# Rows of tiles 4 and 5 through HBM, own PSUM banks for the halves of the first scores and transposes, one buffer for the last output, and a list drawn up anew

## The chip, the cores and the metric

The kernel runs on one core of a Trainium2 chip. The metric is the device time of one execution in microseconds (us), lower is better; it is the median of several executions. TensorE (PE) does the matrix products and the transposes, VectorE (DVE), ScalarE (ACT) and GpSimd (POOL) do the element-wise work, SyncE (SP) issues most of the DMAs, and ACT issues the others. Each engine runs its own instructions in the order of the program.

## The reference

The first part is an attention with a window: for each of 4 batches, 8 heads, 768 positions and 64 columns per head, a query sees the keys nearer than 16 positions and, besides, one summary of each block of 32 positions (the maximum of the keys, the mean of the values). The second part is a two-layer network on the 3072 rows that come out. Cut to what matters:

```python
k_sum = k.reshape(B, H, nb, 32, D).max(axis=3)
v_sum = v.reshape(B, H, nb, 32, D).mean(axis=3)
scores_l = where(|i - j| < 16, scale * q @ k.T, -1e9)
scores_s = scale * q @ k_sum.T + log(32)
a = softmax(concat([scores_l, scores_s]))
x = a @ concat([v, v_sum])            # 3072 rows of 512
h = x @ w_in                          # 512 -> 1024
solu = h * softmax(h)
ln = (solu - mean(solu)) / sqrt(var(solu) + 1e-6) * g_ln
out = ln @ w_out                      # 1024 -> 512
```

All of it is float32. A product of the network is made as three products of rounded parts (high times low, low times high, high times high), so one 128x512 piece is a group of three matmuls.

## The kernel before, in words

The rows are worked on in 24 tiles of 128 rows. One step of the attention, named by batch, part and pair as in `s0_1_0`, makes the rows of half the heads of two tiles: scores `s` (PE), masked and reduced by DVE to `e` and its maximum `nm`, `exp` on ACT with the sums `z`, a division (DVE or POOL), transposes `t` (PE), copies `at` (ACT or DVE), and products with the values `vt` and the block means `vsum` to `x`. The rows are split into a high and a low part, `xh` and `xl`. A tile's first layer is `h` (8 groups of three matmuls; from tile 8 on two tiles are combined into `hu`, `hl` and `hf`), then softmax and normalisation give `he`, and the second layer `o` (8 groups) needs `he` transposed, in the parts `lh` and `ll`. Its result is scaled to `os` by ACT or DVE, and ACT issues the store.

The transposition of `he` has two forms. Tiles 0 to 5 are turned by PE into PSUM (`lt`, line 1130), and ACT and DVE split them from there. Tiles from `FAR_FROM` on are turned in 32x32 blocks by DVE (`tbl`, line 1086), sent to HBM (`farl`, line 1090), fetched back by four DMAs that put the blocks in place (line 1096), and split out of SBUF.

At the start the weights have to be rounded as well: each of 8 pieces of `w_in` (`raw`, `cv`, `w`) takes some seven operations on ACT, DVE and POOL before PE can use it, and the 8 pieces of `w_out` the same.

Nothing of the order is decided on the chip. A planner records each operation with its engine and what it depends on; the table `ORDER` lists all 1890 operations in the order in which the engines get them, `OTHERS` says which run on another engine than the first choice. The planner's own costs serve for one thing only: where they leave PE without work before 80 us, it puts in products of zeros (line 1353, called fillers here), so that PE does not idle. Buffers are rings: a new `s` or `t` takes one of two slots of two PSUM banks each, and must wait until the last tile of that slot is done with.

Of the kernel before, what the change touches and what calls it, by code (L numbers as in the profile page):

```python
# [1397 lines left out]
```

## Time and profile before

| | us |
|---|---|
| median of 3 executions (lowest, highest) | 358.99 (358.83, 360.65) |
| profiled execution | 358.75 |
| span of the profiled execution | 357.0 |
| PE busy in the span | 348.5 |
| DVE busy | 293.2 |
| ACT busy | 264.3 |
| POOL busy | 189.5 |
| DMA moved | 67.80 MB |

The profiled execution's own time is 1.75 us over its span; that part lies outside the rows of the trace. Busy time is a sum over stages with different limits, so it is read stage by stage below.

### The profile page before, as it was taken

What the parts mean: (1) busy time and instruction counts of PE and PEld (TensorE: products, weight loads), DVE (VectorE), ACT (ScalarE), POOL (GpSimd) and SP (SyncE); (2) the same over time, 40 slices, a digit from 0 to 9 for tenths busy, and PEclk for the clock granted to TensorE, in tenths of its full rate; (3) what the DMA queues carried; (4) which work ended last, traced back from release to release, by engine and by line L of the source; (5) the groups of instructions that cost most, each with busy time, mean ns of one, the idle gap of its engine ahead of it and who ended that gap; (6) DMA issues with size and microseconds to landing.
All of it is one profiled execution on the core that took longest, in us unless ns stands there. A gap on an engine that the chain in (4) does not pass through costs nothing.

```text
span 357.0 us, 9393 instructions
## 1 busy us (share of the span) xinstructions
PE 348.5 (98%) x3305; PEld 274.9 (77%) x3311; DVE 293.2 (82%) x969; ACT 264.3 (74%) x780; POOL 189.5 (53%) x330
## 2 busy tenths in 40 slices
PE   8699999999999999999999999999999999999995
PEld 3446667878878888788888888888888888888885
DVE  3889999989899999896878797987988888848421
ACT  4879999978879887889888497797786866654210
POOL 5723446594869859467786345265233353511430
PEclk9999999999999999999999999999999999999999
DMA  7999933745214456286494565683474352354611
GB/s 263 414 413 408 409 142 109 270 119 172 106 46 130 153 206 194 86 287 198 159 311 135 169 211 173 202 251 114 135 228 180 119 170 103 137 176 159 213 70 59
DMA packets 28314, 67.80 MB, mean 190 GB/s; under 512 B 3828, under 2 KB 13300, under 8 KB 26732
## 3 DMA queue, kind: packets, MB, share of 16 engines
q1 hardware_dynamic: 24668, 60.92, 50.2%
q10 hardware_dynamic: 3600, 6.29, 5.0%
q8 instruction: 26, 0.43, 0.5%
q14 instruction: 20, 0.16, 0.2%
HBM read 49.55 MB, written 15.73 MB: 183 GB/s over the span
## 4 chain that ended last, share of the span: by engine, by line
PE 90%; DVE 5%; DMA 2%; issue 1%; ACT 1%; SPq 0%; POOL 0%; DVEq 0%
PE o L1156 37%; PE hu L980 12%; PE h L960 12%; PE x L800 6%; PE hl L980 6%; PE s L676 6%; PE t L741 3%; PE hf L980 3%; DMA kraw<-in_k 2%; DVE e L697 1%; PE vs_ps L557 1%; PE lt L741 1%; DVE ksum L537 1%; DMA out<-os 1%; PE vs_ps L570 1%
## 5 line engine op out<-in xcount | busy, mean ns | idle before, releaser
L1156 PE MATMUL o<-w,lh 128*128 128x512 f32 (+1 forms) x400 | 132.0, 386 | 0.0
L1156 PEld LDWEIGHTS o<-w,lh 128*128 128x128 f32 x400 | 74.1, 188 | 15.6 <-issue 0.5
L1156 PE MATMUL o<-w,ll 128*128 128x512 f32 (+1 forms) x200 | 76.2, 381 | 0.0
L709 ACT ACTIVATE e<-e,nm 128x120 f32<-128x120 f32 x192 | 73.2, 387 | 0.9 <-DVE nm L697 0.8
L960 PE MATMUL h<-w,xh 128*128 128x512 f32 x128 | 44.1, 399 | 0.0
L697 DVE CUSTOM_DVE_ANT_0 e<-s,mask 128x120 f32<-128x120 f32 x192 | 40.7, 276 | 3.4 <-PE s L676 3.4
L1156 PEld LDWEIGHTS o<-w,ll 128*128 128x128 f32 x200 | 37.6, 188 | 6.7
L376 POOL TENSOR_TENSOR ll<-lt,lh 128x512 fp32r<-128x512 f32 x17 | 22.6, 1329 | 37.6 <-ACT lh L368 21.7
L709 ACT ACTIVATION_READ_ACCUMULATOR e<-e,nm 128x1 f32 x192 | 36.9, 192 | 0.0
L960 PEld LDWEIGHTS h<-w,xh 128*128 128x128 f32 x128 | 24.0, 188 | 6.8 <-ACT at L368 0.8
L368 ACT COPY at<-t 120x512 f32<-120x512 f32 x37 | 20.2, 586 | 9.5 <-PE t L741 9.0
L800 PEld LDWEIGHTS x<-at,vt 120*64 120x64 f32 (+1 forms) x768 | 23.9, 138 | 3.8 <-issue 2.9
L1066 ACT ACTIVATE sq<-he 128x1024 bf16<-128x1024 f32 x24 | 25.3, 1055 | 1.8 <-DVE he L1061 0.8
L800 PE MATMUL x<-at,vt 120*64 120x64 f32 (+1 forms) x768 | 26.1, 224 | 0.2 <-POOL cv L476 0.2
L1043 ACT ACTIVATE he<-hs,hm 128x512 f32<-128x512 f32 x24 | 17.2, 718 | 11.8 <-DVE hm L1033 11.8
L1059 POOL TENSOR_SCALAR he<-he,nmu 128x512 f32<-128x512 f32 x19 | 13.5, 714 | 22.4 <-DVE nmu L1054 22.1
L960 PE MATMUL h<-w,xl 128*128 128x512 f32 x64 | 25.0, 391 | 0.0
L368 ACT CAST lh<-lt 128x512 fp32r<-128x512 f32 x35 | 20.5, 610 | 5.9 <-PE o L1156 4.7
L1162 ACT ACTIVATE os<-o,y 128x512 f32<-128x512 f32 x17 | 11.5, 685 | 14.8 <-issue 8.0
L1086 DVE STREAM_TRANSPOSE tbl<-he 128x1024 f32<-128x1024 f32 x18 | 22.3, 1237 | 0.1
L599 POOL TENSOR_TENSOR st_v<-st_v 96x512 f32<-96x512 f32 (+3 forms) x28 | 22.0, 789 | 0.4
L676 PE MATMUL s<-kw,qt 64*64 64x120 f32 x704 | 21.7, 267 | 0.1
(180 smaller groups left out, 842.7 us busy)
## 6 DMA issues: line engine op xcount, KB each, us to landing
vt<-in_v SPq DMA_DIRECT2D x12, 1024.0 KB
farl<-tbl SPq DMA_DIRECT2D x18, 512.0 KB
lt<-farl SPq DMA_DIRECT2D x72, 128.0 KB
kraw<-in_k SPq DMA_DIRECT2D x16, 400.0 KB
out<-os ACTq DMA_DIRECT2D x23, 256.0 KB
qt<-in_q SPq DMA_DIRECT2D x11, 512.0 KB
raw<-in_w_in SPq DMA_DIRECT2D x8, 512.0 KB
raw<-in_w_out SPq DMA_DIRECT2D x8, 512.0 KB
```

The lines of the kernel that those rows point to most:

```text
L368: by = {act: lambda: nc.scalar.copy(out=to(), in_=of()), dve: lambda: nc.vector.tensor_copy(out=to(), in_=of()), pool: lambda: nc.gpsimd.t ...
L376: pool: lambda: nc.gpsimd.tensor_tensor(out=to(), in0=a(), in1=b(), op=kind)}
L599: op(pool, 0.15 + w * 0.0021, lambda w=w, o=o: nc.gpsimd.tensor_tensor(out=o.ap[:n, :w], in0=x.ap[:n, :w], in1=x.ap[:n, w:2 * w], op=ALU.add),
L676: nc.tensor.matmul(sc.ap[cu * QT:(cu + 1) * QT, j, c:c + ks.shape[-1]], qs.ap[ds, 2 * pp + i, u * QT:(u + 1) * QT], ks, start=True, stop=True)
L697: nc.vector.tensor_tensor_reduce(out=e.ap[:, n, :], in0=sc.ap[:, j, (2 * i + up) * KC:(2 * i + up + 1) * KC], in1=mask[:, mi, :], scale=-S ...
L709: nc.scalar.activation(out=e.ap[:, n, :], in_=e.ap[:, n, :], func=AF.Exp, bias=nm.ap[:, n:n + 1], scale=-1.0, accum_out=z.ap[:, n:n + 1])
L800: nc.tensor.matmul(xp()[j * D:(j + 1) * D, i, qs], vs.ap[:k, u, cs], at.ap[:k, u % 2, n[j] + u // 2, :], start=not apart or i == u == 0, s ...
L960: nc.tensor.matmul(hp.ap, a.ap[:, c, ts], w.ap[:, i], start=(c == 0 and n == 0), stop=(c == NKC - 1 and n == 2))
L980: nc.tensor.matmul(to.ap, operand(y, n)[:, c], w(c).ap(i), start=first and c == 0 and k == 0, stop=c == 1 and k == 2, skip_group_check=True)
L1066: op(act, 0.99, lambda: nc.scalar.activation(out=sq.ap, in_=e.ap, func=AF.Square, accum_out=ss.ap), r=[e], w=[sq, ss])
L1086: op(dve, 1.17, lambda: nc.vector.transpose(out=tb.ap.rearrange("p (q c a) -> p q c a", q=4, a=32), in_=of().rearrange("p (c q a) -> p q c ...
L1156: nc.tensor.matmul(o.ap[:, cols], a.ap[:, f, :], w.ap[:, i, cols], start=(f == 0 and n == 0), stop=(f == NFC - 1 and n == 2))
```

## The change

The threshold `FAR_FROM` goes from 6 to 4, so tiles 4 and 5 take the way through HBM. For the two steps of the first scores each half gets its own slot (`scs`), and so do the halves of their transposes (`tp`). The two halves of the last tile's result share one buffer `os`, marked by halves. In the first steps the products with the block means stand ahead of those with the values in one operation, where they were an operation of their own behind. The block means of batch 0 reach `vt` by a DMA on ACT's queue (one per part), where they were two copies on POOL or ACT; the four DMAs of the next batch's means go from SP's queue to ACT's. The first layers of tiles 0 and 1 are no longer interleaved by halves, their PSUM banks are numbered in turn, and the pieces of `w_in` are loaded in another order. Some costs in the planner are changed (they decide where fillers go), and `ORDER` and `OTHERS` are replaced.

```diff
-FIRST_BANKS = (0, 2), (1, 0), (2, 1)
-FAR_FROM = 6
+FAR_FROM = 4
...
-    ORDER = [0, 1, 4, 5, 2, 7, 8, 6, 10, 55, 54, 56, 57, 12, 76, 77, 78, 79, 13, 58, 80, 9, 22, 3, 140, 21, 35, 24,
+    ORDER = [5, 2, 1, 4, 7, 6, 8, 12, 0, 13, 21, 137, 35, 22, 14, 68, 69, 9, 24, 71, 70, 10, 72, 41, 23, 3, 26, 195,
...
-        return bank(FIRST_BANKS[t][half] if t < EARLY else half, "h", f"h{t}_{half}")
+        return bank((2 * t + half) % 3 if t < EARLY else half, "h", f"h{t}_{half}")
...
-            op(sp, 0.75, lambda g=g: nc.sync.dma_start(
+            op(act, 0.75, lambda g=g: nc.scalar.dma_start(
                 out=y.ap[WIN + 6 * g:WIN + 6 * g + 6, :], in_=rows.ap[32 * g:32 * g + 6, :]),
...
-        if not b:
-            for i in range(2):
-                to = lambda i=i: x.ap[WIN:KC, 2 * i:2 * i + 2]
-                of = lambda: y.ap[WIN:KC, :].rearrange("p (o c) -> p o c", o=1).broadcast_to([NB, 2, DM])
-                copy(((pool, 1.1), (dve, 0.62), (act, 0.97)), to, of, r=[y], w=[(x, 1 + i)], port=True)
-            return None
         e, cost, queue = (sp, 0.86, nc.sync) if b else (act, 0.8, nc.scalar)
...
-        sc = plan.buf(ps, [P, 2, 512], F32, "s", 2, "s" + nm_)
+        scs = [plan.buf(ps, [P, 2, 512], F32, "s", 2, f"s{nm_}_{i}") for i in range(1 + each)]
...
-                op(pe, 1.1, lambda i=i: mm(i), r=[(qs, 2 * pp + i), (x, i), (y, i)], w=[(sc, i)], kind="s")
+                op(pe, 1.1, lambda i=i: mm(i), r=[(qs, 2 * pp + i), (x, i), (y, i)], w=[scs[i]], kind="s")
...
-                op(dve, 0.83, lambda i=i: reduce((i,)), r=[(sc, i)], w=[(e, i), (nm, i)])
+                op(dve, 0.83, lambda i=i: reduce((i,)), r=[scs[i]], w=[(e, i), (nm, i)])
...
             for i in range(2):
                 ns = slice(4 * i, 4 * i + 4)
-                op(pe, 0.3, lambda ns=ns: turn_halves(
-                    tp.ap[:KC], lambda n: e.ap[:, n, :], range(8)[ns]), r=[(e, i)], w=[(tp, i)], kind="t")
-                copy(COPY_P, lambda ns=ns: at.ap[:KC, :, ns], lambda ns=ns: tp.ap[:KC, :, ns], r=[(tp, i)], w=[(at, i)])
+                tp = plan.buf(ps, [P, 2, 8, QT], F32, "s", 2, f"t{nm_}_{i}")
+                op(pe, 0.3, lambda ns=ns, tp=tp: turn_halves(
+                    tp.ap[:KC], lambda n: e.ap[:, n, :], range(8)[ns]), r=[(e, i)], w=[tp], kind="t")
+                copy(COPY_P, lambda ns=ns: at.ap[:KC, :, ns], lambda ns=ns, tp=tp: tp.ap[:KC, :, ns], r=[tp], w=[(at, i)])
...
-        if apart:
-            op(pe, 0.98, mm, r=[vs, at], w=[xb], kind="x")
-            op(pe, 0.9, means, r=[vm, at], w=[xb], kind="x")
-        else:
-            yield 0.97, mm, [vs, at], [xb], "x"
+        yield 1.85 if apart else 0.97, mm, [vs, at] + [vm] * apart, [xb], "x"
...
-            os = plan.buf(sb, [P, DM], F32, "os", 2, f"os{t}")
+            if not cols.start:
+                os = plan.buf(sb, [P, DM], F32, "os", 2, f"os{t}")
+            key = os, cols.start
...
-        if t == 0:
-            first(0, (0,))
-            first(1, (0,))
-            first(0, (1,))
-        else:
-            first(t, (1,) if t == 1 else (0, 1))
+        first(t)
```

What the new table moves is shown at three places, in rows of the engines' programs (what is written, what it is made from, the shape). The first is SP's queue at its start: `kraw` are keys, `qt` queries, `raw` pieces of the weights, `st_v` rows of values for the means. Before:

```order
L447 DMA raw_97<-in_w_in 128x1024
L447 DMA raw_98<-in_w_in 128x1024
L621 DMA qt_0_100<-in_q 128x512
L528 DMA kraw_0_153<-in_k 128x800 x2
L528 DMA kraw_1_154<-in_k 128x800
L621 DMA qt_0_100<-in_q 128x512
L528 DMA kraw_1_154<-in_k 128x800
L447 DMA raw_102<-in_w_in 128x1024
L545 DMA st_v_0_104<-in_vr 128x1024
```

Of the change:

```order
L534 DMA kraw_0_153<-in_k 128x800 x2
L454 DMA raw_98<-in_w_in 128x1024
L627 DMA qt_0_100<-in_q 128x512
L534 DMA kraw_1_154<-in_k 128x800 x2
L627 DMA qt_0_100<-in_q 128x512
L551 DMA st_v_0_104<-in_vr 128x1024
```

The first keys now lead, one piece of weights instead of two stands ahead of the first queries, and the first value rows come ahead of the third piece of weights.

The second place is PE between the first scores and the first products with the values: `vs_ps0` are products for the block means, `t0_0_0` and `t0_0_1` transposes of the first two steps (behind the change with the half as a further number), `x0_0_0<-zero` fillers. Before:

```order
L557 MATMUL vs_ps0_231<-st_v0_0_104,sel_162 24x512 x2
L741 MATMUL t0_0_0_387<-ident_68,e0_0_0_155 120x64 x8
L557 MATMUL vs_ps0_231<-st_v0_1_105,sel_162 24x512 x2
L741 MATMUL t0_0_1_409<-ident_68,e0_0_1_156 120x64 x8
L741 MATMUL t0_0_0_387<-ident_68,e0_0_0_155 120x64 x8
L741 MATMUL t0_0_1_409<-ident_68,e0_0_1_156 120x64 x8
L1353 LDWEIGHTS zero_73
L1353 MATMUL x0_0_0_442<-zero_73 128x512
L557 MATMUL vs_ps0_231<-st_v0_2_106,sel_162 24x512 x2
```

Of the change, from the end of the fourth score (`s0_0_1_0`) on; the first `vs_ps0` product stands ahead of that score now:

```order
L676 MATMUL s0_0_1_0_334<-ksum0_1_164,qt0_0_100 64x24
L563 MATMUL vs_ps0_222<-st_v0_1_105,sel_162 24x512 x2
L741 MATMUL t0_0_0_1_377<-ident_68,e0_0_0_155 120x64 x8
L741 MATMUL t0_0_0_0_387<-ident_68,e0_0_0_155 120x64 x8
L563 MATMUL vs_ps0_222<-st_v0_2_106,sel_162 24x512 x2
L741 MATMUL t0_0_1_1_411<-ident_68,e0_0_1_156 120x64 x8
L1339 LDWEIGHTS zero_73
L1339 MATMUL x0_0_0_433<-zero_73 128x512
L741 MATMUL t0_0_1_0_435<-ident_68,e0_0_1_156 120x64 x8
```

The order of the pieces is nearly the same, with one product moved up; twelve fillers follow the last row shown (three followed before), and `x0_0_0` after them.

The third place is the end of ACT's program, where the last stores are issued; a row with 128x256 is a half of tile 23. Before:

```order
L1166 DMA out<-os_5035 128x512
L1166 DMA out<-os_5043 128x512
L1166 DMA out<-os_5109 128x512
L1166 DMA out<-os_5111 128x256
L1166 DMA out<-os_5115 128x256
```

Of the change:

```order
L1158 DMA out<-os_5024 128x512
L1158 DMA out<-os_4946 128x512
L1158 DMA out<-os_5089 128x512
L1158 DMA out<-os_5087 128x256 x2
L1158 DMA out<-os_5093 128x512
```

The last store was a half of tile 23, and is now the whole of tile 22 (`os_5093`), behind both halves.

## Rows read from the trace of the kernel before

**Rows 1.** The page: busy time by engine, with the number of instructions.

```profile
PE 348.5 (98%) x3305; PEld 274.9 (77%) x3311; DVE 293.2 (82%) x969; ACT 264.3 (74%) x780; POOL 189.5 (53%) x330
```

**Rows 2.** Windows: length, then busy us (instructions) of PE, PEld, DVE, ACT, POOL; clock; DMA.

```profile
16.50:351.00 334.50, 333.87 (x3128) 266.34 (x3133) 282.27 (x929) 254.40 (x749) 178.20 (x304) 1.00 0.55 185
...
30.00:66.00 36.00, 35.72 (x409) 25.61 (x412) 34.99 (x130) 35.48 (x107) 19.85 (x24) 1.00 0.66 251
...
140.00:351.00 211.00, 211.00 (x1830) 175.10 (x1830) 165.87 (x549) 147.45 (x439) 99.47 (x193) 1.00 0.52 169
```

**Rows 3.** Timeline of PE, 15 to 25 us: start, us, what, in brackets idle before.

```profile
15.46 0.42 PE L676 MATMUL s<-kraw,qt 64*64 64x96 f32 x8 [1.16 <-DVE nm L697]
16.51 1.90 PE L557 MATMUL vs_ps<-st_v,sel 128*24 128x512 f32 x4 [0.25 <-issue]
24.30 1.15 PE L800 MATMUL x<-at,vt 96*64 96x64 f32 x32
```

**Rows 4.** The chain that ended last, by time: start, us, what.

```profile
10.31 0.83 PE s L676 x17
41.48 1.46 PE x L1353 x6
```

**Rows 5.** Windows of the first 46 us, columns as in rows 2; the last is GB/s.

```profile
1.00:4.00 3.00, 2.75 (x7) 1.01 (x8) 0.19 (x1) 1.27 (x2) 2.63 (x10) 1.00 0.62 175
4.00:10.00 6.00, 5.39 (x54) 2.63 (x52) 3.96 (x7) 2.79 (x4) 2.89 (x6) 1.00 1.00 375
10.00:46.00 36.00, 33.28 (x406) 19.89 (x404) 32.08 (x122) 32.96 (x104) 15.97 (x26) 1.00 1.03 412
```

**Rows 6.** Timeline of DVE, 8 to 13 us, columns as in rows 3.

```profile
8.30 1.96 DVE L537 TENSOR_REDUCE ksum<-kraw 128x24 f32<-128x768 f32 x2
11.16 0.28 DVE L697 CUSTOM_DVE_ANT_0 e<-s,mask 128x120 f32<-128x120 f32 x1 [0.90 <-PE s L676]
11.98 0.95 DVE L537 TENSOR_REDUCE ksum<-kraw 128x24 f32<-128x768 f32 x1
```

**Rows 7.** The chain that ended last, 110 to 165 us: start, us, what.

```profile
113.46 0.68 PE h L960 x3
119.08 0.61 PE t L741 x16
119.69 0.50 PE lt L741 x16
120.20 1.08 PE x L800 x32
121.28 1.01 PE s L676 x32
160.08 2.72 PE o L1156 x12
```

**Rows 8.** Timeline of DVE: tile 6 on its way through HBM.

```profile
126.86 1.23 DVE L1086 STREAM_TRANSPOSE tbl<-he 128x1024 f32<-128x1024 f32 x1
149.04 0.69 DVE L375 TENSOR_TENSOR ll<-lt,lh 128x512 fp32r<-128x512 f32 x1
```

**Rows 9.** Waits of SP's queue: total us, times, longest.

```profile
SPq L1096 <- DVE ll L375: 34.7, 10, 6.1
```

**Rows 10.** The end: PE, DVE (timelines), the store (chain), ACT's issues, the last window.

```profile
353.06 0.28 PE L1156 MATMUL o<-w,lh 128*128 128x256 f32 x1
353.96 0.48 DVE L1164 TENSOR_SCALAR os<-o,y 128x256 f32<-128x256 f32 x1 [0.46 <-DMA out<-os]
351.82 2.02 DMA out<-os
L1166 ACTq DMA_DIRECT2D out<-os x25: 338/338/380, 91.2 to 354.5; - x25
355.50:357.00 1.50, 0.00 (x0) 0.00 (x0) 0.00 (x0) 0.00 (x0) 0.00 (x0) 0.51 0.16 53
```

More of the change, by code (lines that the diff above doesn't have):

```diff
@@ L86 @@
 class Plan:
-    RATES = (6.9, 270.0), (30.0, 410.0), (60.0, 365.0), (1e9, 410.0)
+    RATES = (6.9, 270.0), (30.0, 410.0), (60.0, 390.0), (1e9, 410.0)
     SMALL = 40.0
@@ L300, in order @@
     def order(self):
-        free, dma, held, lock, kind, done = {}, 0.0, 0.0, 0.0, None, set()
+        free, begun, landed, dma, held, lock, kind, done = {}, {}, [0.0] * 8, 0.0, 0.0, 0.0, None, set()
         engine = {i: e for e, those in self.OTHERS.items() for i in those}
@@ L310, in order @@
             o.cost, o.fn = o.can[e]
-            t = o.start = max([free.get(e, self.START)] + [
+            last = free.get(e, self.START)
+            t = o.start = max([landed[-8] if e == "sp" else 0.0, begun.get(e, self.START) if e == "act" and o.nbytes else last] + [
                 d.end + (0.0 if d.engine == e == "pe" else self.SYNC) for d in o.deps])
+            begun[e] = t
             turn = self.TURN if e == "pe" and kind not in (None, o.kind) else 0.0
             other = lock if e == "dve" and o.port else held if e == "pool" else 0.0
-            o.end = free[e] = t + (o.cost + turn) * (2 if e == "pe" and t < self.COLD else 1) + max(other - t, 0.0)
+            o.end = t + (o.cost + turn) * (2 if e == "pe" and t < self.COLD else 1) + max(other - t, 0.0)
             if e == "pe":
                 kind = o.kind
+                if t > 35 and t - last > 0.5:
+                    o.end += min(1.6, 0.7 * (t - last - 0.4)) * (0.6 if t < 80 else 1.0)
+            free[e] = max(last, o.end)
             if e == "dve" and o.port:
@@ L326, in order @@
                 o.end = (own if e == "act" else dma) + (o.land or next(x for t, x in self.LANDS if dma <= t))
+                if e == "sp":
+                    landed.append(o.end)
         return order
@@ L357, in attn_then_solu @@
     ADD_W = ((dve, 0.6), (pool, 1.3))
-    MUL_E = ((pool, 1.9), (dve, 1.07))
+    MUL_E = ((pool, 1.78), (dve, 1.07))
     const = ctx.enter_context(tc.tile_pool(name="const", bufs=1))
@@ L497, in split_w_out @@
         op(act, 0.61, lambda: nc.scalar.activation(out=hl.ap[:, 0], in_=w(), func=AF.Copy, scale=gs),
-           r=[(st, 0), g_b], w=[(hl, 0)], alt=[(dve, 0.36, lambda: nc.vector.tensor_scalar(
-                out=hl.ap[:, 0], in0=w(), scalar1=gs, scalar2=None, op0=ALU.mult))], port=True)
+           r=[(st, 0), g_b], w=[(hl, 0)])
         op(dve, 0.66, lambda: nc.vector.scalar_tensor_tensor(
@@ L640, in load_v2 @@
             out=x.ap[WIN:KC], in_=y.ap[WIN:KC, :].rearrange("p (o c) -> p o c", o=1).broadcast_to([NB, G, DM])),
-            r=[y], w=[(x, 1), (x, 2)], nbytes=NB * 8192 * (4 if b else 1))
+            r=[y], w=[(x, 1)], nbytes=NB * 8192 * (4 if b else 1), land=None if b else 3.3)
     def scores(b, g, pp, direct=False, each=False):
@@ L676, in mm @@
                             nc.tensor.matmul(
-                                sc.ap[cu * QT:(cu + 1) * QT, j, c:c + ks.shape[-1]],
+                                scs[i * each].ap[cu * QT:(cu + 1) * QT, j, c:c + ks.shape[-1]],
                                 qs.ap[ds, 2 * pp + i, u * QT:(u + 1) * QT], ks, start=True, stop=True)
@@ L697, in reduce @@
                 nc.vector.tensor_tensor_reduce(
-                    out=e.ap[:, n, :], in0=sc.ap[:, j, (2 * i + up) * KC:(2 * i + up + 1) * KC],
+                    out=e.ap[:, n, :], in0=scs[i * each].ap[:, j, (2 * i + up) * KC:(2 * i + up + 1) * KC],
                     in1=mask[:, mi, :], scale=-SCALE, scalar=3.0e38,
@@ L712, in scores @@
         for i in range(2):
-            op(act, 1.48, lambda i=i: exps(i), r=[(nm, i) if each else nm], w=[(e, i), (z, i)])
+            op(act, 1.53, lambda i=i: exps(i), r=[(nm, i) if each else nm], w=[(e, i), (z, i)])
         for i in range(2) if each else [None]:
@@ L779, in values @@
         xp = lambda: xb.ap.rearrange("p (i n) -> p i n", i=2)
-        def means():
-            for i in range(2):
-                for j in range(2):
-                    n = 4 * i + 2 * j
-                    cs = slice((4 * pp + 2 * i + j) * D, (4 * pp + 2 * i + j + 1) * D)
-                    nc.tensor.matmul(
-                        xp()[j * D:(j + 1) * D, i, :].rearrange("p (a c q) -> p a c q", a=2, c=2),
-                        vm.ap[:KC, cs], at.ap[:KC, :, n:n + 2, :].rearrange("p c a q -> p a c q"),
-                        start=False, stop=i == 1, skip_group_check=True)
         def mm():
@@ L795, in mm @@
                 n = [4 * i + 2 * j for j in range(2)]
+                if apart:
+                    for j in range(2):
+                        cs = slice((4 * pp + 2 * i + j) * D, (4 * pp + 2 * i + j + 1) * D)
+                        nc.tensor.matmul(
+                            xp()[j * D:(j + 1) * D, i, :].rearrange("p (a c q) -> p a c q", a=2, c=2),
+                            vm.ap[:KC, cs], at.ap[:KC, :, n[j]:n[j] + 2, :].rearrange("p c a q -> p a c q"),
+                            start=i == 0, stop=False, skip_group_check=True)
                 for u in range(G):
@@ L801, in mm @@
                             xp()[j * D:(j + 1) * D, i, qs], vs.ap[:k, u, cs], at.ap[:k, u % 2, n[j] + u // 2, :],
-                            start=not apart or i == u == 0, stop=not apart, skip_group_check=apart)
-        if apart:
-            op(pe, 0.98, mm, r=[vs, at], w=[xb], kind="x")
-            op(pe, 0.9, means, r=[vm, at], w=[xb], kind="x")
-        else:
-            yield 0.97, mm, [vs, at], [xb], "x"
+                            start=not apart, stop=not apart or u == G - 1, skip_group_check=apart)
+        yield 1.85 if apart else 0.97, mm, [vs, at] + [vm] * apart, [xb], "x"
         if NG * b + g >= FAST:
@@ L945, in sums_end, with first @@
             keep(4, c)
-    def first(t, halves=(0, 1)):
+    def first(t):
         b, g, j = t // (2 * NG), (t // 2) % NG, t % 2
         ts = slice(j * P, (j + 1) * P)
+        hs = [place_h(t, i) for i in range(2)]
         hi, lo = xh[b, g], xl[b, g]
-        hs = begun_h.setdefault(t, [])
-        for c, nh in [(c, nh) for nh in halves for c in range(NKC)]:
-            if c == 0:
-                hs.append(place_h(t, nh))
+        for c, nh in sorted(w_in_pieces, key=lambda x: x[::-1]):
             w, hp = wt[c * 2 + nh], hs[nh]
@@ L963, in first @@
             op(pe, 0.6805, mm, r=[(hi, c), (lo, c), w], w=[hp])
-        if len(hs) == 2:
-            solu(t, [(lambda hp=hp: hp.ap, hp) for hp in hs])
+        solu(t, [(lambda hp=hp: hp.ap, hp) for hp in hs])
     def first_two(t, behind, turns, rest=True):
@@ L1065, in solu @@
         sq = plan.buf(sb, [P, DF], BF16, "sq", 1, f"sq{t}")
-        op(act, 0.99, lambda: nc.scalar.activation(
+        op(act, 1.05, lambda: nc.scalar.activation(
             out=sq.ap, in_=e.ap, func=AF.Square, accum_out=ss.ap), r=[e], w=[sq, ss])
-        mul = lambda to, x: op(pool, 0.18, lambda: nc.gpsimd.tensor_tensor(out=to.ap, in0=to.ap, in1=x.ap, op=ALU.mult), r=[x], w=[to])
-        op(pool, 0.18, lambda: nc.gpsimd.tensor_scalar(
+        mul = lambda to, x: op(pool, 0.22, lambda: nc.gpsimd.tensor_tensor(out=to.ap, in0=to.ap, in1=x.ap, op=ALU.mult), r=[x], w=[to])
+        op(pool, 0.25, lambda: nc.gpsimd.tensor_scalar(
             out=ss.ap, in0=ss.ap, scalar1=1.0 / DF, scalar2=1e-6, op0=ALU.mult, op1=ALU.add), w=[ss])
@@ L1160, in second_parts @@
                 yield
-            os = plan.buf(sb, [P, DM], F32, "os", 2, f"os{t}")
+            if not cols.start:
+                os = plan.buf(sb, [P, DM], F32, "os", 2, f"os{t}")
+            key = os, cols.start
             op(act, 0.12 + 0.47 * k, lambda o=o, os=os, cols=cols: nc.scalar.activation(
                 out=os.ap[:, cols], in_=o.ap[:, cols], func=AF.Copy, scale=y.ap),
-               r=[o, y], w=[os], alt=[(dve, 0.06 + 0.54 * k, lambda o=o, os=os, cols=cols: nc.vector.tensor_scalar(
+               r=[o, y], w=[key], alt=[(dve, 0.06 + 0.6 * k, lambda o=o, os=os, cols=cols: nc.vector.tensor_scalar(
                    out=os.ap[:, cols], in0=o.ap[:, cols], scalar1=y.ap, scalar2=None, op0=ALU.mult))])
             op(act, 0.42, lambda os=os, cols=cols: nc.scalar.dma_start(
-                out=out[t * P:(t + 1) * P, cols], in_=os.ap[:, cols]), r=[os], nbytes=int(P * 2048 * k))
+                out=out[t * P:(t + 1) * P, cols], in_=os.ap[:, cols]), r=[key], nbytes=int(P * 2048 * k))
     its = [(b, g) for b in range(B) for g in range(NG)]
@@ L1174, in attn_then_solu @@
         "w": [lambda c=c, nh=nh: load_w(c * 2 + nh, w_in[c * P:(c + 1) * P, nh * 512:(nh + 1) * 512])
-              for c, nh in sorted(w_in_pieces, key=lambda x: x[::-1])],
+              for c, nh in w_in_pieces],
         "r": [lambda i=i: load_v_rows(0, i) for i in range(3)],
@@ L1195, in attn_then_solu @@
             run(values(0, 0, i // 2, 0, True))
-    load_v2(*its[1])
-    begun = []
+    begun = [load_v2(*its[1])]
     for i in range(3):
```

29 lines of the change are left out of this document (13 added, 16 removed), and 198 rows, old and new, of tables (ORDER, OTHERS).

## The prediction

> **What bounds the kernel now.** I read the busy times first: PE is busy 348.5 of 357.0 us, DVE and ACT 293.2 and 264.3 [rows 1]. A share over the whole span says little, so I went on to windows. From 16.5 to 351 us PE idles 334.50 - 333.87 = 0.63 us, and from 140 us on not at all [rows 2]. The transpose on DVE, the way through HBM and the second layer are therefore hidden in the later part, and a change there counts only as work of PE taken away or as a new wait. Three things can move the end: PE's own work, the head before 16.5 us, and the tail after PE's last product at 353.34 (353.06 + 0.28) [rows 10]. There is one warning: from 30 to 66 us DVE is busy 34.99 and ACT 35.48 of 36 us [rows 2]. There PE's fillers stand where PE would otherwise wait for those two.
>
> The timeline of PE shows what the head waits for. The fourth half of the first scores starts at 15.46 after a wait of 1.16 us for DVE's `nm`, and the first product for the block means only at 16.51 [rows 3]. Transfers set the start: the core moves 175 GB/s from 1 to 4 us, 375 up to 10 us and 412 up to 46 us [rows 5].
>
> **The head: 4.1 us earlier.** Bytes from the shapes of SP's rows: ahead of the first scores stood two pieces of weights (0.52 MB each), two keys (0.41 each) and a query (0.26), 2.13 MB; now it is one piece less, 1.61 MB. By the rates, 0.525 MB are in at 4 us, so the last of them comes at 4 + 1.08/0.375 = 6.9 us, where it was 8.3, just when DVE's first maximum starts (8.30) [rows 6]. I let the query land at 7.5, as some time goes by between the transfer and its signal.
>
> From there I walk the new order with the old durations: a half of scores 0.83 [rows 4], a key maximum 0.95, and the masking of a half 11.98 - 11.16 = 0.82 [rows 6]. The first two halves run from 7.6 to 8.4, the second step's maximum to 9.4, three maskings end at 10.25, 12.0 (another maximum lies between) and 12.85. The third half runs from 10.4 to 11.25. Since each half has its own slot, the fourth needs no slot later than 12.0. PE takes the first means product (1.90 [rows 3]) from 11.5 to 13.5, in time that it idled away before, and the fourth half ends at 14.35. Before, scores and this product were done at 16.51 + 1.90 = 18.4. The lead at equal work is 18.4 - 14.35 = 4.05, say 4.1 us; 1.4 of it come from the loads, the rest from that idle time.
>
> The lead isn't kept whole: 26 fillers followed that product, and 30 do now. One is 1.46/6 = 0.24 us [rows 4], so four more cost 1.0. Twelve of them stand before `x0_0_0`, where three did; it starts at 22.5 by the walk, against 24.30 [rows 3]. The value rows `vt` that it needs end at 7.41 MB in both orders, by the rates at 10 + (7.41 - 2.775)/0.412 = 21.3 us, so they don't make it later. After `x0_0_0` five fewer fillers stand than before.
>
> Moving DMAs off SP and copies off POOL costs PE nothing by itself. An issue takes ACT 0.338 us [rows 10], four of them 1.35 in a stage where ACT is full; in return about seven conversions of weights go to POOL, which is busy 19.85 of 36 us there [rows 2]. I set this at nothing. If that cover is gone, ACT's casts come late by up to 1.35, and PE by as much; ACT also waits once for the load of the second part's `vt` with exps behind it, and the walk leaves about 1 us there.
>
> The Trainium skill ("DMA: Bandwidth & Descriptors", "Issuing engines are not separate DMA queues") says that a DMA runs on the same engines whichever engine issues it, and that spreading the issue saves only the time on the issuing sequencer. By that the moved DMAs gain no bandwidth, and the sum keeps its nothing. [...]
>
> **The middle: 1.0 us.** PE no longer turns `he` of tiles 4 and 5. One such turn, 16 transposes, stands in the chain at 119.69 with 0.50 us [rows 7]; one per tile goes, 2 x 0.50 = 1.0. All other products of PE are the same in number. DVE gets two `tbl` of 1.23 us [rows 8], and loses part of the splits out of PSUM; after 66 us it has room, so nothing.
>
> **The tail: 0.4 us worse.** The last `os` waited 0.46 us for a store [rows 10], and with its own buffer it doesn't. But the last store is now a whole tile, issued behind both halves. With E for PE's end at 353.34: before, the last `os` ended at 353.96 + 0.48 = E + 1.10; then came one issue of 0.34 and a store of 128 KB, which I bound by half of a whole store's 2.02 and by all of it: E + 2.45 to E + 3.46. Now: 0.16 from E to the scaling (0.62 less the wait of 0.46), 0.48 for it, two issues of 0.34, and a whole store of 2.02 [rows 10], E + 3.34. The loss lies between -0.1 and 0.9; I take the middle, 0.4.
>
> **Sum.** 4.1 - 1.0 + 1.0 - 0.4 = 3.7 us. The profiled execution's own time is 358.75, span 357.0 and 1.75 around it; it stands 0.24 below the median of 358.99. 358.75 - 3.7 = 355.05, so 355.1.
>
> **Rivals.** *The lead is swallowed.* DVE and ACT have no free time from 30 to 66 us [rows 2], so a head that starts earlier can end no earlier, unless their work moves too. For: 0.52 and 1.01 us free in 36. Against: seven conversions leave ACT, two `vt` copies go, and DVE works earlier as well, as its first idle time of 0.90 was a wait for scores [rows 6]. In between, going by the work of DVE needed ahead of PE's points, I get a lead of 2.5 instead of 4.1. Whole, the rival leaves 1.0 - 0.4 = 0.6 us: 358.1.
>
> *Rows of tile 4 come late: slower.* The way through HBM takes tile 6 from the end of its last `h` group (113.46 + 0.68 = 114.14) to the end of `ll` (149.04 + 0.69 = 149.73) 35.6 us [rows 7, 8]; it had until 160.08, 10 us more than needed. Between the last `h` group of tile 4 and its first `o` the new order has 32 groups of 0.68, four `t` of 0.61, four `s` of 1.01, three `x` of 1.08, one turn of 0.50 [rows 7] and five changes of kind of 0.25 [rows 3]: 33.2 us of PE's work. At the pace of tile 6, `o4` would wait 35.6 - 33.2 = 2.4 us. Tile 5 has 36 groups, and about 2 us more. For this rival: DVE and ACT are fuller here than at 114 us, and fetches on SP wait up to 6.1 us for `ll` in ten places [rows 9]. Against: much of tile 6's 35.6 us is queueing behind other work, not transfer, and the planned order may put it ahead. With 2.4 the sum is 357.5, still a gain; with one further wait of 6.1, 8.5 us and the half clock after it (below, I put two groups, 1.4, on it), 355.1 + 9.9 = 365. It ends on the slower side once the way takes more than 33.2 + 3.7 = 36.9 us.
>
> The half clock: in the last window, PE having had no work since 353.34, the granted clock is 0.51, the 1.2 GHz level, where it is 1.00 elsewhere [rows 10]. The Trainium skill ("TensorE: Matmul & The Clock Gate", "HAM oscillation — how this bites in real kernels") has PE throttled again by waits for DMA between pieces of work. The trace agrees at its end; in the middle no wait there is so long, so no row shows the price of coming back. By the skill a wait for `o4` would cost more than itself.
>
> *The walk was too slow.* If the query lands at 6.9 (0.6 sooner) and the 0.63 us of idle time [rows 2] go as well: 355.1 - 1.2 = 353.9; with a tail that costs nothing, 353.5.
>
> **How the numbers follow.** My forecast has 0.60, its own range 354 to 357.2: the lead down to 2.5 gives 356.7, the tail's bounds 0.5 to either side. The swallowed lead has 0.18, the walk too slow 0.14, rows late 0.08. Less than 0.5%, 1.8 us, can't be told from no change here, so faster means below 357.2. Faster: 0.60 + 0.14, and a small part of rows late, 0.75; same: the swallowed lead, 0.18; slower: 0.07. The range reaches from 352.8 (the walk too slow, and in the tail and the walk 0.7 more) to 358.4 (the swallowed lead, with the tail 0.3 worse).
>
> **What would show it.** In the profile of the changed kernel: the first scores start near 7.6 us and the means product ends by 13.5, the fourth half near 14.35; `x0_0_0` near 22.5; PE idles less than 1 us between there and 351; no wait of `o4` or `o5` for `lh` or `ll`; the last store is a whole tile and ends about 3.3 us behind PE's last product. The forecast is wrong if PE shows waits for `w`, `at` or `vsum` of more than 1 us in sum from 20 to 66 us (lead swallowed), or one of some us at about 80 to 100 us, with a granted clock of 0.5 behind it (rows late).

## The result, and the profile after

The changed kernel takes 362.02 us (median of 6 executions, 361.83 to 362.76), the kernel before 358.94 in the same runs: 1.0076 times as long, 95% interval 1.0056 to 1.0096. It is 3.1 us slower, where 3.7 us less was predicted, and outside the range. The profiled execution is the longest of the six (362.76); its span is 361.0 us, 4.0 more than before, so some 0.7 us of what its rows show isn't in the median.

The page of the changed kernel, its first line of busy times ([rows 1] before):

```profile
PE 348.1 (96%) x3274; PEld 273.1 (76%) x3274; DVE 296.2 (82%) x966; ACT 265.8 (74%) x785; POOL 195.1 (54%) x326
```

PE works as long as before (348.1 against 348.5), so the 4 us are idle time. The windows of the changed kernel (columns as in [rows 2]) say where:

```profile
30.00:66.00 36.00, 35.27 (x349) 25.47 (x348) 34.49 (x131) 34.25 (x103) 20.94 (x24) 1.00 0.78 283
140.00:355.00 215.00, 212.58 (x1840) 175.19 (x1838) 169.33 (x546) 152.94 (x448) 105.46 (x188) 1.00 0.54 168
355.00:361.00 6.00, 0.00 (x0) 0.00 (x0) 1.14 (x2) 0.00 (x0) 0.00 (x0) 0.70 0.36 129
```

The last one has 6 us without any work of PE, with 1.14 us of DVE in them. Of the 2.42 us without PE in the second one, 1.88 lie behind its last product (353.12, below); the other 0.54 are new, as PE idled not at all there before [rows 2], and 0.4 of them is a wait of `hu` for `hs`. The timeline of PE in the changed kernel (start, us, what, in brackets the idle time before) gives the head and the last product:

```profile
9.04 0.42 PE L676 MATMUL s<-kraw,qt 64*64 64x96 f32 x8 [1.04 <-DMA qt<-in_q]
...
12.02 0.42 PE L676 MATMUL s<-kraw,qt 64*64 64x96 f32 x8 [0.85 <-DVE nm L697]
...
13.22 1.88 PE L563 MATMUL vs_ps<-st_v,sel 128*24 128x512 f32 x4
15.03 0.42 PE L676 MATMUL s<-kraw,qt 64*64 64x96 f32 x8
...
21.25 2.76 PE L1339 MATMUL x<-zero 128*128 128x512 bf16 x12
23.95 0.65 PE L790 MATMUL x<-at,vsum 120*64 120x256 f32 x4
...
28.14 1.05 PE L676 MATMUL s<-kw,qt 64*64 64x120 f32 x32 [0.38 <-DMA qt<-in_q]
...
32.21 1.05 PE L676 MATMUL s<-kw,qt 64*64 64x120 f32 x32 [0.54 <-DVE nm L697]
...
352.84 0.28 PE L1146 MATMUL o<-w,lh 128*128 128x256 f32 x1
```

PE's last product ends at 353.12, 0.22 us before the old 353.34 [rows 10]; 4.1 us had been forecast for this point (the lead of 3.1 that the fillers leave, and 1.0 of turns). From there to the end of the span it is 7.88 us now and was 3.66. So two things failed, each by close to 4 us: the tail costs 4.2 more instead of 0.4, and PE gains 0.2 instead of 4.1.

The timeline of DVE in the changed kernel, the last two lines:

```profile
352.96 1.14 DVE L1156 TENSOR_SCALAR os<-o,y 128x256 f32<-128x256 f32 x2 [9.24 <-PE o L1146]
356.25 1.14 DVE L1156 TENSOR_SCALAR os<-o,y 128x512 f32<-128x512 f32 x2 [2.15 <-DMA out<-os]
```

DVE sits idle for 9.24 us, waiting for PE's last tile, and then has four scalings to do, two of them of whole tiles; before the third it waits 2.15 us for a store. (A line here groups neighbours under the shape of the first.) The end of DVE's program shows why, by the numbers of the tiles' rows:

```
L1156 TENSOR_SCALAR os_5087<-o_5041,y_4923 128x256
L1156 TENSOR_SCALAR os_5089<-o_4894,y_4821 128x512
L1156 TENSOR_SCALAR os_5093<-o_4999,y_4871 128x512
L1156 TENSOR_SCALAR os_5087<-o_5034,y_4923 128x256
```

`os_5089` is tile 20, whose product was done long before; it stands behind the first half of tile 23 (`os_5087`). `os_5093` is tile 22, which takes the slot of tile 20 in the ring of two and so waits for tile 20's store. The second half of tile 23, whose product ended at 353.12, is queued behind both. The chain that ended last, in the changed kernel, has the store:

```profile
354.13 2.02 DMA out<-os
```

### The profile page after: what moved, and what is told of

Its sections match the earlier page's. It is cut to its first block, busy times and chain, and to the rows that moved or that the text cites. A ratio compares the mean times of both kernels' runs of the same rounds, so it can differ in the third digit from the quotient of the medians.

```text
span 361.0 us, 9323 instructions
## 1 busy us (share of the span) xinstructions
PE 348.1 (96%) x3274; PEld 273.1 (76%) x3274; DVE 296.2 (82%) x966; ACT 265.8 (74%) x785; POOL 195.1 (54%) x326
## 4 chain that ended last, share of the span: by engine, by line
PE 76%; DMA 10%; DVE 4%; ACT 3%; POOL 3%; issue 1%; SPq 1%; DVEq 0%; ACTq 0%
PE o L1146 32%; PE h L951 12%; PE hu L970 10%; DMA raw<-in_w_in 5%; PE x L798 5%; PE hl L970 5%; PE s L676 5%; PE t L741 3%; DMA st_v<-in_vr 2%; PE hf L970 2%; DMA lt<-farl 2%; POOL ll L383 1%; DVE e L697 1%; ACT e L709 1%; DVE cv L474 1%
## 5 line engine op out<-in xcount | busy, mean ns | idle before, releaser
L383 POOL TENSOR_TENSOR ll<-lt,lh 128x512 fp32r<-128x512 f32 x21 | 28.0, 1337 | 22.4 <-DVE lh L376 16.8
L383 POOL TENSOR_TENSOR e<-e,z 128x960 f32<-128x960 f32 (+1 forms) x13 | 22.8, 1758 | 27.0 <-DVE z L718 22.7
L375 ACT COPY at<-t 120x512 f32<-120x512 f32 x38 | 21.1, 586 | 14.3 <-PE t L741 13.2
L1076 DVE STREAM_TRANSPOSE tbl<-he 128x1024 f32<-128x1024 f32 x20 | 24.7, 1236 | 3.1 <-POOL he L1049 1.8
L375 ACT CAST lh<-lt 128x512 fp32r<-128x512 f32 x33 | 19.7, 611 | 6.7 <-PE o L1146 5.7
L383 POOL TENSOR_TENSOR xl<-sums,xh 128x256 fp32r<-128x256 f32 (+1 forms) x9 | 8.4, 938 | 29.8 <-DVE xh L376 14.2
L1053 ACT ACTIVATE he<-he,nmu 128x512 f32<-128x512 f32 x25 | 17.9, 721 | 8.7 <-DVE nmu L1044 8.7
L676 PEld LDWEIGHTS s<-kw,qt 64*64 64x64 f32 x704 | 18.2, 133 | 5.2 <-issue 3.1
```

Of the source, the lines that this page charges most:

```text
L375: by = {act: lambda: nc.scalar.copy(out=to(), in_=of()), dve: lambda: nc.vector.tensor_copy(out=to(), in_=of()), pool: lambda: nc.gpsimd.t ...
L383: pool: lambda: nc.gpsimd.tensor_tensor(out=to(), in0=a(), in1=b(), op=kind)}
L676: nc.tensor.matmul(scs[i * each].ap[cu * QT:(cu + 1) * QT, j, c:c + ks.shape[-1]], qs.ap[ds, 2 * pp + i, u * QT:(u + 1) * QT], ks, start=T ...
L1053: (act, 0.62, lambda sl=sl: nc.scalar.activation(out=e.ap[:, sl], in_=e.ap[:, sl], func=AF.Identity, bias=nmu.ap))], port=True)
L1076: op(dve, 1.17, lambda: nc.vector.transpose(out=tb.ap.rearrange("p (q c a) -> p q c a", q=4, a=32), in_=of().rearrange("p (c q a) -> p q c ...
```

## The experiments

Times are medians beside the kernel before in the same runs; where runs taken at different times are compared, it is by their ratios to it. "Mended tail" is the second run's list.

**1. Tile 20 out of the way.** Two entries of `ORDER` move: 1840 and 1841 are tile 20's scaling and store, 1805 tile 18's store, 1876 and 1877 tile 22's scaling and store, 1886, 1887, 1896 and 1897 those of tile 23's halves.

```diff
-1859, 1805, 1874, ..., 1895, 1886, 1840, 1841, 1887, 1876, 1896, 1897, 1877
+1859, 1805, 1840, 1841, 1874, ..., 1895, 1886, 1887, 1876, 1896, 1897, 1877
```

> The changed kernel with one scaling and its store moved: tile 20's os, which stood on DVE behind the first half of tile 23's, goes ahead, right behind the issue of tile 18's store. Theory (a queue in the tail): os of tile 22 waits for tile 20's store, which starts only behind PE's last product, so the tail is 7.9 us where it was 3.7; with tile 20 out of the way it is about 4.1 (three scalings of 0.4, 0.75 and 0.4, issues, a whole store of 2.0), and the time falls by 3.5 to 4 us, to 358.0 to 358.6. Rival (the stores at the end are slow by themselves, or the end is set elsewhere): less than 1 us, 361 or more.

Measured: ratio 0.9996 (0.9979 to 1.0013), or 358.8 us, 3.2 us under the changed kernel and 0.2 above what I had expected. The two entries are worth about three quarters of what run 2 gets back. Of this run only the time is used.

**2. Tile 22 as well.**

```diff
-..., 1879, 1875, 1880, ..., 1886, 1887, 1876, 1896, 1897, 1877
+..., 1879, 1875, 1876, 1877, 1880, ..., 1886, 1887, 1896, 1897
```

> As the run before, and also tile 22's os and store ahead of both halves of tile 23. Theory: the last store is a half again, the tail is 2.7 to 3.0 us, the time 356.8 to 357.6, 4.5 to 5 us under the changed kernel. Rival: as before, little.

Measured: 357.86 us, ratio 0.9969 (0.9956 to 0.9982), 4.16 us under the changed kernel. DVE's timeline of this run:

```profile
349.87 0.75 DVE L1157 TENSOR_SCALAR os<-o,y 128x512 f32<-128x512 f32 x1 [2.82 <-PE o L1147]
353.15 0.88 DVE L1157 TENSOR_SCALAR os<-o,y 128x256 f32<-128x256 f32 x2 [2.54 <-PE o L1147]
```

The last two scalings run without a gap; the 0.46 us for a store between them [rows 10] is gone, as predicted of the one buffer. PE's last product ends at 353.41 and the span at 357.0, a tail of 3.59 us. I had expected 0.6 to 0.9 us less: not even the tail before (3.66) was as short as my walk has it (2.45 to 3.46).

**3 and 4. No fillers behind 30 us of the planner's clock**, with the mended tail, and in the kernel before. Sixteen fillers fewer in each.

```diff
-    COLD, FILL = 6.9, 80.0
+    COLD, FILL = 6.9, 30.0
```

> The tail of the run before, and no fillers behind 30 us of the planner's clock (16 fewer). Theory S (what PE gains early is swallowed, as DVE and ACT are full from 30 to 66 us and the fillers only stand where PE would wait): within 0.7 us of the run before, with new waits of PE in place of the fillers. Theory F (the fillers hold PE up where nothing would make it wait): 16 x 0.24 = 3.8 us faster, about 353.3. A clock that falls in the new waits would make it slower than the run before.

> The kernel before without the fillers behind 30 us of the planner's clock (16 fewer). Theory S: within 0.7 us of before. Theory F: up to 3.8 us faster, 355.1.

Measured: 356.88 us, ratio 0.9935 (0.9913 to 0.9957), and 358.80 us, ratio 0.9996 (0.9981 to 1.0010). In the kernel before theory S holds to the letter: PE's last product ends at 353.34 as before, and waits have taken the fillers' place, as the waits of PE in that run show (what for, total us, times, longest):

```profile
PE h L960 <- DVE he L1051: 1.3, 1, 1.3
...
PE s L676 <- DVE hm L1040: 0.7, 1, 0.7
...
PE x L800 <- POOL vt L370: 0.4, 1, 0.4
```

In the changed list it holds for part of them: 1.0 us comes back by the medians, of 3.8 paid. PE's last product ends at 351.18 there (350.90 + 0.28), 2.2 us before the old 353.34:

```profile
350.90 0.28 PE L1147 MATMUL o<-w,lh 128*128 128x256 f32 x1
```

Run 7 asks which part that is.

**5. The first query earlier.** In SP's queue (5 and 2 are the first keys, 4 the query, 1 a piece of the weights), on the list of run 3:

```diff
-    ORDER = [5, 2, 1, 4, 7, 6, ...
+    ORDER = [5, 4, 2, 1, 7, 6, ...
```

> The run without fillers behind 30 us (and with the mended tail), and the first query's DMA moved two places up, to the second in SP's queue. Theory W (the head's start is carried to the end): the first scores, which waited for the query until 9.0 us, start at 7.5 to 8.2, and the time falls by as much, 0.8 to 1.5 us, to 355.4 to 356.1. Theory S (DVE and ACT swallow it): the first scores move and the time doesn't, within 0.5 of 356.9.

Measured: 357.80 us, ratio 0.9963 (0.9951 to 0.9976), some 1 us slower than run 3, with intervals that just overlap. PE's timeline:

```profile
7.90 0.38 PE L677 MATMUL s<-kraw,qt 64*64 64x96 f32 x2
9.52 0.23 PE L677 MATMUL s<-ksum,qt 64*64 64x24 f32 x1 [1.24 <-DVE ksum L544]
```

The query came in time, but PE then waited for the maximum of the keys behind it. The first scores were done no sooner, so the run doesn't decide between W and S; this order only trades one transfer for the other.

**6. The halves of the first scores share a slot again**, on the list of run 3.

```diff
-        scs = [plan.buf(ps, [P, 2, 512], F32, "s", 2, f"s{nm_}_{i}") for i in range(1 + each)]
+        sc = plan.buf(ps, [P, 2, 512], F32, "s", 2, "s" + nm_)
```

> The run without fillers behind 30 us, and the two halves of the first scores share a slot again, as before the change. If the own slots give nothing, or hold the third half up (it waited 0.85 us for the first half's masking): same or up to 0.5 us faster, 356.4 to 356.9. If they give the means product its place beside the wait, as the prediction has it: about 1 us slower, 357.9.

Measured: 357.56 us, ratio 0.9961 (0.9939 to 0.9983), by the ratios 0.9 us slower than run 3, with intervals that overlap. What the own slots give is therefore not shown. The profiled execution's query landed sooner (8.17 us, where it was 9.34 in run 3) though the loads stand in the same order.

**7 and 8. Fillers up to 62 us, and up to 16 us**, with the mended tail (`FILL` 62.0 and 16.0).

> The mended tail with the fillers up to 62 us and without the five behind it, between 66 and 80 us. Theory F (there PE has work in hand and a filler is paid in full): 5 x 0.24 = 1.2 us faster than the mended tail with all, 356.7. Theory S (they stand in waits): no change, 357.9.

> The mended tail and no fillers behind 16 us, so also the 12 (2.8 us) ahead of the first product with the values are gone. If that product waits for nothing else, it starts up to 2.8 us sooner, at 21.5 us, and the time falls below the run without fillers behind 30 us, to 355 or so. If it waits for its inputs, which is what the fillers cover, nothing, 356.5 to 357.2; slower if the clock falls in the wait.

Measured: 357.04 us, ratio 0.9945 (0.9928 to 0.9963), and 358.09 us, ratio 0.9957 (0.9936 to 0.9978). By the ratios, run 7 is 0.9 us faster than run 2, and run 3, with eleven fillers fewer still, another 0.4; each time the intervals overlap. The timelines of PE help further, at a piece of `h` ahead of the five fillers and at the transposes of a step's `e` behind them. Run 2, then run 7:

```profile
68.23 0.39 PE L952 MATMUL h<-w,xh 128*128 128x512 f32 x1
...
72.97 0.69 PE L742 MATMUL t<-ident,e 64*120 64x64 f32 x16
```

```profile
52.96 0.50 PE L952 MATMUL h<-w,xh 128*128 128x512 f32 x1 [0.28 <-DVE he L1042]
...
67.29 0.39 PE L952 MATMUL h<-w,xh 128*128 128x512 f32 x1
...
71.54 0.69 PE L742 MATMUL t<-ident,e 64*120 64x64 f32 x16 [0.18 <-DVE e L383]
```

Behind the five, run 7 is 1.43 us ahead, but 0.94 of it stood there before them; so the five cost 0.5 us, of 1.2 at 0.24 each. The 0.94 isn't the fillers' doing, as both runs have the same ones up to 62 us. Run 7 was 0.36 us ahead from the third half of the scores on (11.93 and 12.29), and in run 2, as in the changed kernel, DVE waited 0.62 us for a piece of weights until 29.61, and the scores that wait for its `nm` began at 32.47; in runs 7 and 3 that wait is absent, and they began at 31.05 and 30.99. The eleven before 66 us stood in waits: without them the wait for `he` at 53 us is 1.30 us instead of 0.28 (run 3, shown at run 12), and run 3 is 0.24 us ahead of run 7 there (52.72) and 0.23 at 71 us (71.31).

In run 8 PE waits where the twelve fillers stood, and longer than they took (PE's timeline, then a window of it: length, busy time, granted clock, DMA share, GB/s):

```profile
23.49 1.12 PE L791 MATMUL x<-at,vsum 120*64 120x256 f32 x4 [2.98 <-ACT vsum L568]
```

```profile
24.00:26.00 2.00, 2.00 (x24) 0.50 1.04 412
```

The granted clock falls to 0.50, the 1.2 GHz level, behind the wait of 2.98 us, and the product takes 1.12 us where it takes 0.65 in the other runs. That is the price for which the prediction had no row. The Trainium skill ("TensorE: Matmul & The Clock Gate", "HAM oscillation — how this bites in real kernels") describes such a loss behind waits for DMA. Here PE waited for a copy on ACT, and the trace agrees that the work behind the wait ran at the lower clock.

**9. Tiles 4 and 5 turned by PE again**, on the list of run 3 (`FAR_FROM = 6`, the turns ahead of the products `x` of batch 1's second group, the splits right behind them, all else in the order of run 3).

> The run without fillers behind 30 us, with tiles 4 and 5 turned by PE again, as before the change (two turns of 0.50 us come back on PE, two transposes of 1.23 us leave DVE; the order is otherwise the same, the turns stand ahead of the products with the values of the second batch's second step). If PE is the bound there, as the prediction has it: 1.0 us slower than that run, 357.9. If the way through HBM cost as much in other places: no change, 356.9. If DVE's load of it was felt: faster.

Measured: 370.49 us, ratio 1.0315 (1.0298 to 1.0332). New waits of PE between 120 and 150 us drown what was asked; two of them in its timeline:

```profile
121.68 0.50 PE L1138 MATMUL o<-w,lh 128*128 128x512 f32 x1 [1.61 <-ACT os L1146]
...
140.42 0.83 PE L733 MATMUL t<-ident,e 64*120 64x64 f32 x16 [3.73 <-POOL e L375]
```

The question stays open in this run: the list was made for the other way.

**10 and 11. A later head.** The DMA of the first value rows (0.52 MB, entry 12) goes to the front of SP's queue, on the list of run 3 and on that of run 4.

```diff
-    ORDER = [5, 2, 1, 4, 7, 6, 8, 12, ...
+    ORDER = [12, 5, 2, 1, 4, 7, 6, 8, ...
```

> The run without fillers behind 30 us, with the first value rows' DMA (0.52 MB, 1.3 to 1.4 us of transfer) moved to the front of SP's queue, so that the first scores come later by that and all transfers behind them at the old time. Theory W (the head's start is carried to the end): 1.3 us slower, 358.2. Theory S (waits for DVE and ACT further on swallow it): within 0.5 us, 356.9 to 357.4, the wait at 52 us shrinking by what the head lost.

> The same in the kernel before (without fillers behind 30 us): the first value rows' DMA at the front. Theory W: 1.3 us slower than that kernel, 360.1. Theory S: within 0.5 us, 358.8 to 359.3.

Measured: 357.12 us, ratio 0.9949 (0.9934 to 0.9964), some 0.5 us slower than run 3; and 359.78 us, ratio 1.0024 (1.0004 to 1.0044), 1.0 us slower than run 4. Both pairs of intervals overlap, so the times don't tell the two kernels apart. In the traces PE's last product ends 0.71 us later than in run 3 (351.89), where the first product of `x` was 1.01 later, and 1.14 later than in run 4 (354.48), where the fourth half of the scores was 1.34 later (17.09 and 15.75). By these traces both kernels pass most of a late head on to the end.

**12. An earlier head.** ACT copies the block means (39) ahead of a conversion of weights (96), and three fillers fewer stand ahead of the first product; on the list of run 3.

```diff
-... 83, ..., 96, ..., 39, ...        COLD, FILL = 6.9, 30.0
+... 83, ..., 39, 96, ...             COLD, FILL = 6.9, 22.7
```

> The run without fillers behind 30 us, with the copy of the block means on ACT one place up, ahead of a conversion of weights of 0.7 us, and three fillers fewer ahead of the first product, which waits for that copy. The first product starts 0.7 us sooner, at about 23.0. Theory W: 0.7 us faster, 356.2. Theory S: the same within 0.4.

Measured: 357.50 us, ratio 0.9963 (0.9947 to 0.9979): no gain, rather 0.6 us more than run 3, with intervals that overlap. PE's timelines show it step by step: the first product of `x`, the next scores that wait for `nm`, the `h` that waits for `he`. Run 3:

```profile
24.04 0.65 PE L791 MATMUL x<-at,vsum 120*64 120x256 f32 x4
...
30.99 1.05 PE L677 MATMUL s<-kw,qt 64*64 64x120 f32 x32 [0.34 <-DVE nm L698]
...
52.72 0.50 PE L952 MATMUL h<-w,xh 128*128 128x512 f32 x1 [1.30 <-DVE he L1042]
```

Run 12, with the earlier head:

```profile
23.14 0.65 PE L791 MATMUL x<-at,vsum 120*64 120x256 f32 x4
...
30.97 1.05 PE L677 MATMUL s<-kw,qt 64*64 64x120 f32 x32 [1.10 <-DVE nm L698]
...
52.64 0.50 PE L952 MATMUL h<-w,xh 128*128 128x512 f32 x1 [1.28 <-DVE he L1042]
```

Run 6, whose query landed early:

```profile
23.25 0.65 PE L791 MATMUL x<-at,vsum 120*64 120x256 f32 x4 [0.33 <-ACT vsum L568]
...
31.66 1.05 PE L677 MATMUL s<-kw,qt 64*64 64x120 f32 x32 [1.71 <-DVE nm L698]
...
52.92 0.50 PE L952 MATMUL h<-w,xh 128*128 128x512 f32 x1 [1.30 <-DVE he L1042]
```

Run 10, with the later one:

```profile
25.05 0.65 PE L791 MATMUL x<-at,vsum 120*64 120x256 f32 x4
...
31.91 1.05 PE L677 MATMUL s<-kw,qt 64*64 64x120 f32 x32 [0.46 <-DVE nm L698]
...
53.31 0.50 PE L952 MATMUL h<-w,xh 128*128 128x512 f32 x1 [1.28 <-DVE he L1042]
```

A first product 0.9 us sooner (run 12) is 0.02 sooner at 31 us and 0.08 at 53; the wait for `nm` grows by 0.76 in its place. DVE sets that point: it masks those scores from 29.14 us on in run 3 and from 29.12 in run 12, behind other work in both. Run 6 is less clear, as its DVE waited 0.34 us for a piece of weights just ahead of that masking. A first product 1.0 us later (run 10) is 0.9 later at 31 us and still 0.6 at 53. Run 3 stands at the edge: more lead is swallowed, less is felt.

**13. Less work for DVE.** The list of run 12, and two additions of the conversion of `w_in` on DVE left out (the low bits of two pieces are missing, so only the time counts).

```diff
             done.add(o)
-            o.fn()
+            if o.prio not in (93, 100):
+                o.fn()
```

> The run with the copy of the block means moved up, and two additions of the conversion of w_in (two pieces, 0.6 to 0.69 us each, at 24 to 27 us on DVE) left out, so the weights of these pieces lack their low bits and only the time is read. If DVE's own work without a gap from 19 to 36 us is what swallows an early start of PE: the scores that wait for nm until 31.0 us, whether PE is there at 30.6 or at 29.9, start 0.8 to 1.2 us sooner, the wait for he ends near 51.5 instead of 52.7, and the time falls by about 1 us, to 356.4. If the wall is ACT or the transfers: these two points stay, and so does the time, 357.5.

Measured: 356.87 us, ratio 0.9945 (0.9926 to 0.9963) against 0.9963 (0.9947 to 0.9979) of run 12; the intervals overlap. In the trace the two points didn't come sooner: the scores start at 31.77 and the `h` at 53.26. DVE had a wait that run 12 lacks (its timeline):

```profile
29.40 0.60 DVE L476 TENSOR_SCALAR cv<-raw 128x512 int32<-128x512 int32 x1 [1.10 <-DMA raw<-in_w_in]
```

PE had also waited for the second queries, until 28.20, for 1.01 us. But the changed kernel, with all of DVE's work, has the same wait (its DVE), and so have runs 2 and 5:

```profile
29.34 1.11 DVE L474 TENSOR_SCALAR cv<-raw 128x512 int32<-128x512 int32 x1 [0.62 <-DMA raw<-in_w_in]
```

So the run doesn't tell what DVE's work alone is worth: the time that it won was lost in waiting for a transfer that came late in other traces too. It shows that DVE isn't the only thing that holds the head; at 28 to 30 us the transfers stand right behind it.

**14. Rows of tiles 4 and 5 through HBM alone**, in the kernel before (`FAR_FROM = 4`; `tbl` and its store where `he` is done, the rest in the old order).

> The kernel before with the rows of tiles 4 and 5 through HBM as the only change: the two turns of 0.50 us leave PE, two transposes of 1.23 us come onto DVE where he is done, the fetches stand behind the store of each on SP. If PE is the bound there and the way is quick enough, 1.0 us faster, 357.9 to 358.1. If tile 4 or 5 come late (35.6 us for tile 6 before, against 33 to 35 us of PE's work), a wait of o4 or o5 of 2 us or more and a time above before.

Measured: 362.78 us, ratio 1.0104 (1.0087 to 1.0121). In the profiled execution PE's clock fell (PE's timeline, and a window of PE alone):

```profile
17.18 2.98 PE L559 MATMUL vs_ps<-st_v,sel 128*24 128x512 f32 x4 [0.47 <-POOL e L378]
```

```profile
16.00:18.00 2.00, 1.53 (x29) 0.50 1.02 410
```

The means product takes 2.98 us instead of 1.90 [rows 3]. That doesn't explain the median: this execution took 364.13 us at a mean granted clock of 0.993, the other three 362.76 to 362.80 at 0.998 to 1.00. Behind 120 us PE has four waits that the kernel before lacks, 0.58 us of `h` for `he`, 1.00 of `o` for `os`, 0.37 of `hl` for `hs` and 0.43 of `s` for `at`. No `o` waits for `lh` or `ll`, so the rows came in time. In this order the way through HBM is a loss of 3.8 us, and in the trace these waits are 2.4 of it; what it is worth in an order made for it stays open.

## Why the prediction was wrong

**The tail: the step that failed most.** The prediction has "the last store is now a whole tile, issued behind both halves", and E + 3.34 us. I had read ACT's queue, where the stores are issued, and not DVE's, where the scalings stand. There tile 20's scaling stands behind one that needs PE's last tile, with DVE idle for 9.24 us ahead of it, and tile 22's waits for tile 20's store. Measured E + 7.88, 4.2 us more than before, where the prediction's bounds were -0.1 and 0.9. Runs 1 and 2 show it: 4.16 us come back when these four entries move. The one buffer for the last output did what the prediction says of it, as run 2 shows.

**The head: the first query and the second keys.** "By the rates, 0.525 MB are in at 4 us, so the last of them comes at 4 + 1.08/0.375 = 6.9 us", 7.5 with the signal. It came at 9.04. I had taken SP's queue for a pipe that gives up its transfers one after the other. By 9 us the core had moved 8 us x 277 GB/s = 2.2 MB (a window from 1 to 9 us of the changed kernel), where 1.61 MB stood ahead of the query and with it: transfers issued behind it had run beside it. The keys behind the query were late too, and they held the third half. It waits for the first masking, and in DVE's program that stands behind the second step's maximum. The walk runs this maximum from 8.4 to 9.4 and doesn't ask when its keys land; DVE waited for them until 10.16:

```profile
10.16 0.95 DVE L543 TENSOR_REDUCE ksum<-kraw 128x24 f32<-128x768 f32 x1 [0.67 <-DMA kraw<-in_k]
11.03 0.27 DVE L697 CUSTOM_DVE_ANT_0 e<-s,mask 128x120 f32<-128x120 f32 x1
```

By this order an earlier query alone would have moved nothing behind it. In run 5 the query came at 7.90, that maximum began at 10.89, and the third half at 12.74, 1.85 us behind it; here it is 1.86. The rest of the walk holds up from there. The third half waited for the masking as walked (12.02, 1.6 later than the walk), the fourth ended at about 15.8 (1.5 later), `x0_0_0` began at 23.95 (1.45 later). The term of 4.1 us was 2.6 at that point.

**The head: what becomes of a lead.** "The lead isn't kept whole", but I took only the extra fillers from it, at 0.24 us each. `x0_0_0` starts 0.35 us before the old 24.30; with 1.2 for five fewer fillers behind it and 1.0 for the turns, PE's end should have come 2.5 us sooner, and it came 0.22 sooner. By this sum some 2.3 us are lost on the way. New waits show for part of them: 0.38 us for the second queries, 0.54 for `nm`, 0.18 for `he`, and 0.43 of `hu` for `hs` behind 140 us, against 0.63 us of idle time from 16.5 us on before [rows 2]; what took the rest no run shows. Run 12 shows how a lead at 24 us is lost by 31 us: DVE, with work in hand, masks the next scores no sooner. In the changed kernel itself DVE waited there for a transfer (run 13). A later head isn't swallowed so: most of it is still there at 31 us and at the end (run 10). This is the rival "the lead is swallowed", which I gave 0.18. I had its rows, DVE and ACT full from 30 to 66 us [rows 2], and argued it down with DVE's starting earlier.

**The fillers.** Four more at 0.24 us was the wrong sum. In the kernel before, the last sixteen cost nothing (run 4); in the changed list eleven of the sixteen behind 30 us cost 0.2 to 0.4 us together and the five behind 66 us 0.5 to 0.9, by the trace and by the ratios (run 7). With them out and the tail mended, the list is 0.65% faster than before (run 3), 2.1 us at these medians, and PE's last product comes 2.2 us sooner: of the forecast 4.1 us at PE's end about half, and it holds the turns that left PE.

**The middle and the rival of late rows.** No wait of `o4` or `o5` is in the changed kernel's trace, so the rows of tile 4 came in time. That the two turns are worth 1.0 us isn't shown: runs 9 and 14 were both blurred by other waits. Nor did a run test what the DMAs moved to ACT's queue cost or gain, which the prediction sets at nothing; the rows before can't show it, as up to 46 us all transfers of that kernel are issued by SP.

## What to carry to other kernels

Read the end of every engine's program that the last output passes, not only the queue of the stores: an operation that has long been ready costs its whole chain when it stands behind one that waits for the last product. A lead at the start is worth what the next full engine or transfer leaves of it, so look for the first wait that stays in place when the head moves, and try it in both directions. Work put in to keep an engine busy is free only where a wait would stand; take it out and see which of it comes back as a wait. And when two traces are compared at a point behind an edit, take off what they differed by ahead of it: of the 1.43 us behind five fillers, 0.94 stood ahead of them.
